# Keys times values for a pair of units and its tail in one go, in a fused attention and experts kernel

## The chip, the cores and the metric

The kernel runs on one core of one Trainium2 chip. The metric is device microseconds of one execution, the median of several. The core's engines are TensorE (PE in the profile; PEld is its weight load), VectorE (DVE), ScalarE (ACT), GpSimd (POOL) and SyncE (SP, which here issues DMAs). Each works through its own instructions in program order and waits for semaphores of the others.

## The reference

Linear attention over 4 batches, 8 heads, 576 tokens and head size 64, with 128 features, then a mixture of 8 experts (two per token), then a plain two-layer network. All is float32. The part that the change touches is `kv` and `z`:

```python
def phi(x):
    proj = np.einsum('bhsd,df->bhsf', x, w_phi)
    proj = proj - np.max(np.abs(proj), axis=-1, keepdims=True)
    return np.concatenate([np.exp(proj), np.exp(-proj)], axis=-1)
q_p, k_p = (phi(q), phi(k))
kv = np.einsum('bhsf,bhsd->bhfd', k_p, v)
z = np.sum(k_p, axis=2)
num = np.einsum('bhsf,bhfd->bhsd', q_p, kv)
den = np.einsum('bhsf,bhf->bhs', q_p, z)[..., None] + 1e-06
# x = num / den -> experts: top-2 of 8, w1, relu, w2 -> relu(x @ w_in)**2 @ w_out
```

## The kernel before

The first 290 us or so are the attention with the router's work strewn in, the rest are the experts and the last network.

A batch has 576 tokens: 512 in four rows of 128 and a tail of 64. Its keys are worked in 9 units. Unit 0 of a batch is the tail of all 8 heads; units 1 to 8 are half of a pair of heads each (pair `p`, half `f`, so units 2p + 1 and 2p + 2). One slot of the loop over `n` (line 786 on) works one unit at each stage of a pipeline written out by hand: `k_a(n + 1)` transposes keys, `k_b(n)` multiplies them with `w_phi` and lets VectorE take the maximum (`kmx`), the difference (`kd`) and ScalarE the two exponentials (`k_e`, into `kp`, or into `kpt` for a tail), and `k_c(n - 1)` adds keys times values and the sums over tokens into one bank of PSUM (`KV`), where they stay until the pair is complete; then VectorE copies the bank to `kvz`, and `k_d` turns it for the queries two slots later (`kvc`). The queries run beside: `q_a0` splits them into a high and a low part (`qhl`; ScalarE and VectorE), `q_a` transposes, `q_b` projects, POOL takes the maximum over features, `q_c1` and `q_c2` subtract and take exponentials, `q_d` multiplies with `kvc` and `norm` divides. On TensorE a slot's order is `k_a`, `q_a`, `k_b`, `q_b`, `k_d`, the router's few matmuls or none, `k_c`, `q_d`, `q_tail`.

`k_c` today: for the first unit of a pair (`f == 0`) it issues keys times values (tiles of 128 rows by 64 columns, two at once), sums (a stationary of ones, 128 by 32, four at once), then the pair's tail times values (64 by 64, since a tail's four heads of one kind have 64 partitions) and the tail's sums (64 by 32). For the second unit it issues the first two again and the copy. A unit of a tail issues nothing. A matmul of float32 shows as two passes, so `x8` in the trace are four matmuls.

The tail's values `vtt` are loaded with four heads in partitions 0 to 63 and four in 64 to 127, so a pair of heads has 64 rows. Values wait in three buffers `vt`: `load_v` (line 238, called at 796) of a pair waits on SP's queue until `k_c` has read the pair three earlier. SP's queue also holds, in program order, loads of keys and queries, the clears of the experts' input (`clear`, `xg_d<-zero`) and the experts' first weights (`w_load` in slots 6, 8, ... 20 and up, `w_conv` in the slot after, on ScalarE and VectorE).

Router: groups of tokens go through `r_0` to `r_6` over some eight slots, nearly all small VectorE work; `r_3b` puts ranks into one of the two banks `N0`, `N1` that `q_d` uses too, and `r_4` reads them.

Of the kernel before, what the change touches and what calls it, by code (L numbers as in the profile page):

```python
# [30 lines left out]
def kernel(  # L31
# [107 lines left out]
    def x_tile(pt, shape, dt, tag, small, bufs=1):  # L139
        if pt == 0:  # L140
            return xp[0].tile(shape, dt, name=tag + "0", tag=small[0], bufs=small[1])
        return xp[0].tile(shape, dt, name=tag, tag=tag, bufs=bufs)
# [5 lines left out]
    def x_load(pt):  # L148
        e, j0, j1 = parts[pt]
        if e == E - 1:  # L150
            j1 = NJ
        src = xg_d[e * CAP:e * CAP + CAP].rearrange("(j p) d -> p j d", p=128)
        if pt == 1:
            for j in range(j0, j1):
                t = stage.tile([128, DM], FT, name="xs", tag="wstage", bufs=WST)
                nc.sync.dma_start(t, src[:, j])
                XG[pt, j] = t
        else:
            t = x_tile(pt, [128, JA if pt == 0 else NJ, DM], FT, "xg", ("qhlt", 1))
            nc.sync.dma_start(t[:, :j1], src[:, :j1])  # L160
            for j in range(j1):
                XG[pt, j] = t[:, j]

    def x_t(pt, j):
        e = parts[pt][0]
        if pt not in XT:
            n = RA if pt == 0 else CAP
            XT[pt] = (x_tile(pt, [128, DC, n], FR, "xth", ("kp", 2)), x_tile(pt, [128, DC, n], FR, "xtl", ("kp", 2)))
            if pt == NP - 2:
                XT[pt + 1] = XT[pt]  # L170
        t = bank(["Tk", "M0", "M1"][j % 3], [128, DC, 128])
        for d in range(DC):
            nc.tensor.transpose(t[:, d], XG[pt, j][:, d * 128:d * 128 + 128], ident)  # L173
        c = x_cols(pt, j)
        hi_lo(XT[pt][0][:, :, c], XT[pt][1][:, :, c], t)
# [51 lines left out]
    with ExitStack() as actx:  # L227
# [26 lines left out]
            QT[b, h] = t  # L254

        def load_tails(b):
            t = ap_.tile([TL, H, D], FT, name="ktt", tag="ktt", bufs=2)
            nc.sync.dma_start(t, _ap(k, b * H * S * D + SM * D, [[D, TL], [S * D, H], [1, D]]))
            KTT[b] = t
            if b == 0:  # L260
                load_k(0, 0)
            t = ap_.tile([TL, H, D], FT, name="qtt", tag="qtt", bufs=1)
            nc.sync.dma_start(t, _ap(q, b * H * S * D + SM * D, [[D, TL], [S * D, H], [1, D]]))
            QTT[b] = t
            t = ap_.tile([128, 4, D], FT, name="vtt", tag="vtt", bufs=2)
            for s in range(2):
                nc.sync.dma_start(t[s * 64:(s + 1) * 64],
                                  _ap(v, (b * H + 4 * s) * S * D + SM * D, [[D, TL], [S * D, 4], [1, D]]))
            VTT[b] = t

# [22 lines left out]
        spare = ap_.tile([128, NTILE, 2], FT, name="spare", tag="spare")  # L293


        wf = ap_.tile([128, 128], FT, name="wf", tag="wf")
        nc.sync.dma_start(wf, _ap(w_phi, 0, [[0, 2], [128, 64], [1, 128]]))
        load_tails(0)
# [5 lines left out]
        nc.sync.dma_start(gw[:, :, 0, :], _ap(w_gate, 0, [[E, 128], [128 * E, 4], [1, E]]))  # L304
        nc.sync.dma_start(gw[:, :, 1, :], _ap(w_noise, 0, [[E, 128], [128 * E, 4], [1, E]]))

        jp = ap_.tile([128, 128], I32, name="jp", tag="jp")
        nc.gpsimd.iota(jp, pattern=[[1, 128]], base=0, channel_multiplier=-1)
        nc.vector.tensor_scalar(ident, jp, 0.0, None, op0=OP.is_equal)
        nc.scalar.activation(identr, ident, AF.Copy)  # L310
# [52 lines left out]
        def k_b(u):  # L363
            b, i = divmod(u, 9)
            hi, lo = KH.pop(u)
            t = bank(f"M{u % 2}", [128, 2, 2, 128])
            for r in range(2):
                o = t[:, r].rearrange("p h f -> p (h f)")
                s = slice(r * 128, r * 128 + 128)
                mm(o, hi[:, s], wbh, r == 0, False)  # L370
                mm(o, hi[:, s], wbl, False, False)
                mm(o, lo[:, s], wbh, False, True)
            mx = ap_.tile([128, 4], FT, name="kmx", tag="kmx", bufs=2)
            nc.vector.tensor_reduce(mx, t.rearrange("p r h f -> p (r h) f"), axis=AX.X, op=OP.max,  # L374
                                    apply_absolute_value=True)
            kd = ap_.tile([128, 4, 128], FT, name="kd", tag="kd", bufs=2)
            nc.vector.tensor_sub(kd, t.rearrange("p r h f -> p (r h) f"),
                                 mx[:, :, None].to_broadcast([128, 4, 128]))
            if i == 0:
                kp = ap_.tile([128, 4, 2, 128], FT, name="kpt", tag="kpt", bufs=1)  # L380
                KPT[b] = kp
            else:
                kp = ap_.tile([128, 4, 2, 128], FT, name="kp", tag="kp", bufs=2)
                KP[u] = kp
            KE.append((kp, kd))

# [3 lines left out]
            nc.scalar.activation(kp[:, :, 1, :], kd, AF.Exp, scale=-1.0)  # L390

        def k_c(u):
            b, i = divmod(u, 9)
            if i == 0:
                return
            p, f = divmod(i - 1, 2)
            if f == 0:
                KVB[b, p] = bank("KV", [128, 512])
            t = KVB[b, p]
            kp = KP.pop(u).rearrange("p (h r) a f -> p r h (a f)", h=2)  # L400
            for r in range(2):
                for h in range(2):
                    mm(t[h * 64:h * 64 + 64, :256], VT[b, p][:, h, 2 * f + r, :], kp[:, r, h],
                       f == 0 and r == 0, f == 1 and r == 1)
            for h in range(2):
                for r in range(2):
                    g = 32 * (2 * h + r)
                    mm(t[g:g + 32, 256:], ones32, kp[:, r, h], False, f == 1)
            if f == 0:
                rows = slice((p // 2) * 64, (p // 2) * 64 + 64)  # L410
                kt = KPT[b].rearrange("p (r h) a f -> p r h a f", h=2)
                for h in range(2):
                    mm(t[h * 64:h * 64 + 64, :256], VTT[b][rows, (p % 2) * 2 + h, :],
                       kt[rows, p % 2, h].rearrange("p a f -> p (a f)"), False, False)
                for h in range(2):
                    for a in range(2):
                        g = 32 * (2 * h + a)
                        mm(t[g:g + 32, 256 + a * 128:384 + a * 128], ones32[rows], kt[rows, p % 2, h, a], False, False)
            else:
                kvz = ap_.tile([128, 512], FT, name="kvz", tag="kvz", bufs=1)  # L420
                nc.vector.tensor_copy(kvz, t)
                KVZ[b, p] = kvz

        def k_d(u):
            b, i = divmod(u, 9)
# [15 lines left out]
        def q_a0(u):  # L441
            b, i = divmod(u, 9)
            if i == 0:
                s = ap_.tile([TL, H, 2, D], FR, name="qhlt", tag="qhlt", bufs=1)
                hi_lo(s[:, :, 0, :], s[:, :, 1, :], QTT[b])
            else:
                s = ap_.tile([128, R, 2, D], FR, name="qhl", tag="qhl", bufs=2)
                hi_lo(s[:, :, 0, :], s[:, :, 1, :], QT[b, i - 1])
            QHL[u] = s

        def q_a(u):
            b, i = divmod(u, 9)
            t = bank("Tq", [128, 512], FR)
            s = QHL.pop(u)
            if i == 0:
                for h in range(H):
                    nc.tensor.transpose(t[:, h * 64:h * 64 + 64],
                                        s[:, h].rearrange("p a d -> p (a d)"), identr[:64, :64])
            else:
                for r in range(R):  # L460
                    nc.tensor.transpose(t[:, r * 128:r * 128 + 128],  # L461
                                        s[:, r].rearrange("p a d -> p (a d)"), identr)
            o = ap_.tile([128, 512], FR, name="qtr", tag="qtr", bufs=2)
            nc.scalar.activation(o, t.bitcast(FT), AF.Copy)
            QTR[u] = o

        def q_b(u):
            t = bank("P", [128, 512])
            o = QTR.pop(u)
            mm(t, wsh, o, True, False)  # L470
            mm(t, wsl, o, False, True)
            ps = ap_.tile([128, 512], FT, name="ps", tag="ps", bufs=3)
            nc.scalar.activation(ps, t, AF.Copy)  # L473
            mx = ap_.tile([128, 512], FT, name="qmx", tag="qmx", bufs=3)
            nc.gpsimd.partition_all_reduce(mx, ps, 128, bass.bass_isa.ReduceOp.absmax)  # L475
            PS[u] = (ps, mx)

# [784 lines left out]
```

## Time and profile before

| what | us |
|---|---|
| median of three runs | 1144.59 (1144.57 to 1145.79) |
| profiled execution | 1142.34 |
| its span, first to last instruction | 1140.6 |
| TensorE busy in the span | 1101.5 (97%) |
| VectorE busy | 642.7 (56%) |
| ScalarE busy | 493.8 (43%) |
| GpSimd busy | 396.8 (35%) |
| mean granted clock of TensorE, share of full | 0.987 |

Times are of one profiled execution unless they are called medians. A matmul's end is modelled, so groups of matmuls are read from the start of one to the start of the next. A table of windows gives, for a stretch, its length and each engine's busy time in it; an engine whose busy time equals the length never waited. "Idle before" in brackets, with an arrow, is how long an engine waited and what ended the wait.

### The profile page before, as it was taken

What the parts mean: (1) busy time and instruction counts of PE and PEld (TensorE: products, weight loads), DVE (VectorE), ACT (ScalarE), POOL (GpSimd) and SP (SyncE); (2) the same over time, 40 slices, a digit from 0 to 9 for tenths busy, and PEclk for the clock granted to TensorE, in tenths of its full rate; (3) what the DMA queues carried; (4) which work ended last, traced back from release to release, by engine and by line L of the source; (5) the groups of instructions that cost most, each with busy time, mean ns of one, the idle gap of its engine ahead of it and who ended that gap; (6) DMA issues with size and microseconds to landing.
All of it is one profiled execution on the core that took longest, in us unless ns stands there. A gap on an engine that the chain in (4) does not pass through costs nothing.

```text
span 1140.6 us, 17665 instructions
## 1 busy us (share of the span) xinstructions
PE 1101.5 (97%) x6588; PEld 935.0 (82%) x6588; DVE 642.7 (56%) x1247; ACT 493.8 (43%) x1025; POOL 396.8 (35%) x374
## 2 busy tenths in 40 slices
PE   7999889989999999999999999999999999999996
PEld 4676667678889999999999988888898888888885
DVE  6778778775148687878777774343343333333222
ACT  5767567641453535444445354443233232222221
POOL 3333342743545454545454545553010010000000
PEclk9999999998999999999999999999999999999998
DMA  5768352614646555555555555332112011001001
GB/s 133 223 178 263 89 168 65 208 75 173 224 142 199 180 193 183 193 178 189 179 194 180 196 182 164 122 109 74 37 39 55 19 38 56 19 1 37 1 1 40
DMA packets 106366, 142.51 MB, mean 125 GB/s; under 512 B 17570, under 2 KB 59682, under 8 KB 105762
## 3 DMA queue, kind: packets, MB, share of 16 engines
q1 hardware_dynamic: 100514, 122.44, 33.9%
q0 software_dynamic: 5760, 18.88, 5.1%
q8 instruction: 54, 0.88, 0.3%
q14 instruction: 38, 0.31, 0.1%
HBM read 92.97 MB, written 48.31 MB: 124 GB/s over the span
## 4 chain that ended last, share of the span: by engine, by line
PE 86%; DVE 6%; DMA 2%; issue 2%; ACT 1%; another core or an unknown queue 1%; POOL 1%; SPq 0%; POOLq 0%
PE M L81 38%; PE N L81 16%; PE KV L81 12%; PE P L81 9%; PE Tq L81 8%; DVE qhl L85 1%; PE Tk L81 1%; PE Tq L461 1%; PE M L173 1%; DMA wstage<-in_moe_w_dram 1%; DVE kmx L374 1%; PE Tk L995 1%; PE Tk L173 1%; PE Tk L356 1%
## 5 line engine op out<-in xcount | busy, mean ns | idle before, releaser
L1016 DVE TENSOR_TENSOR r<-M,r 128x512 f32<-128x512 f32 (+1 forms) x80 | 51.0, 638 | 245.1 <-ACT h2h L1015 242.3
L1012 ACT ACTIVATE r<-M 128x512 f32<-128x512 f32 (+1 forms) x80 | 44.4, 555 | 247.7 <-PE M L81 245.5
L202 ACT ACTIVATE hh<-M 128x320 fp32r<-128x320 f32 (+2 forms) x128 | 50.8, 437 | 227.7 <-PE M L81 220.6
L199 DVE SCALAR_TENSOR_TENSOR hl<-M,hh 128x320 fp32r<-128x320 f32 (+2 forms) x128 | 58.1, 486 | 114.7 <-ACT hh L202 113.4
L475 POOL PARTITION_ALL_REDUCE qmx<-ps x36 | 69.9, 1942 | 137.0 <-ACT ps L473 132.7
L977 POOL DMA_INDIRECT ya<-y_d,yrows x18 | 17.9, 997 | 187.2 <-PE Tk L995 112.5
L81 PEld LDWEIGHTS N<-kvc,qp 128*128 128x128 f32 x512 | 62.1, 197 | 17.5 <-issue 11.9
L81 PE MATMUL N<-kvc,qp 128*128 128x81 f32 x512 | 67.0, 284 | 9.5 <-issue 4.2
L1017 DVE TENSOR_TENSOR h2l<-r,h2h 128x512 fp32r<-128x512 f32 (+1 forms) x80 | 57.7, 721 | 7.3 <-DVE r L1016 0.5
L1015 ACT ACTIVATE h2h<-r 128x512 fp32r<-128x512 f32 (+1 forms) x80 | 47.1, 589 | 2.6
L81 PE MATMUL M<-x,w30h 128*128 128x512 f32 (+1 forms) x160 | 45.9, 371 | 0.0
L81 PE MATMUL M<-x,w20h 128*128 128x512 f32 (+1 forms) x160 | 45.7, 370 | 0.0
L81 PE MATMUL M<-x,w10h 128*128 128x512 f32 (+1 forms) x160 | 45.7, 370 | 0.0
L81 PE MATMUL M<-x,w00h 128*128 128x512 f32 (+1 forms) x160 | 45.4, 368 | 0.0
L128 POOL TENSOR_TENSOR w30l<-wstage,w30h 128x512 fp32r<-128x512 f32 x20 | 27.4, 1370 | 49.9 <-ACT w30h L127 47.4
L128 POOL TENSOR_TENSOR w20l<-wstage,w20h 128x512 fp32r<-128x512 f32 x20 | 28.0, 1399 | 45.0 <-ACT w20h L127 29.4
L740 POOL DMA_INDIRECT xg_d<-x,slots x32 | 31.9, 997 | 21.7 <-DVE slots L701 11.8
L85 DVE TENSOR_TENSOR qhl<-qt,qhl 128x256 fp32r<-128x256 f32 x32 | 37.0, 1156 | 0.4 <-ACT qhl L84 0.4
L128 POOL TENSOR_TENSOR w10l<-wstage,w10h 128x512 fp32r<-128x512 f32 x16 | 22.3, 1394 | 40.6 <-ACT w10h L127 36.8
L947 POOL TENSOR_TENSOR wd<-wd 128x256 f32<-128x256 f32 x32 | 23.7, 741 | 36.0 <-DVE wd L943 31.7
L947 POOL TENSOR_TENSOR wx<-wx 128x256 f32<-128x256 f32 x32 | 23.7, 740 | 35.1 <-DVE wx L943 31.6
L952 DVE SCALAR_TENSOR_TENSOR wd<-wd 128x256 f32<-128x256 f32 x32 | 35.1, 1096 | 1.1
(439 smaller groups left out, 3465.0 us busy)
## 6 DMA issues: line engine op xcount, KB each, us to landing
wstage<-in_moe_w_dram SPq DMA_DIRECT2D x128, 256.0 KB
xg_d<-zero SPq DMA_DIRECT2D x8, 1280.0 KB
y_d<-y SPq DMA_DIRECT2D x40, 256.0 KB
xg<-xg_d SPq DMA_DIRECT2D x7, 1280.0 KB
wide<-in_moe_w_in_dram SPq DMA_DIRECT2D x32, 256.0 KB
wide<-in_moe_w_out_dram SPq DMA_DIRECT2D x32, 256.0 KB
kt<-in_k_dram SPq DMA_DIRECT2D x16, 256.0 KB
vt<-in_v_dram SPq DMA_DIRECT2D x16, 256.0 KB
```

Source lines behind the costliest of these rows:

```text
L81: nc.tensor.matmul(o, l, r, start=start, stop=stop, skip_group_check=True)
L85: nc.vector.tensor_sub(lo, src, hi.bitcast(FT))
L128: (nc.gpsimd if n >= 2 else nc.vector).tensor_sub(lo[:, c], src, hi[:, c].bitcast(FT))
L199: nc.vector.scalar_tensor_tensor(hl[:, c0:c1], o, 0.0, hh[:, c0:c1].bitcast(FT), op0=OP.max, op1=OP.subtract)
L202: nc.scalar.activation(hh[:, c[1]:c[2]], c[0], AF.Relu)
L475: nc.gpsimd.partition_all_reduce(mx, ps, 128, bass.bass_isa.ReduceOp.absmax)
L947: nc.gpsimd.tensor_mul(part, part, exp)
L952: nc.vector.scalar_tensor_tensor(exp, ok, TINY * TINY, exp, op0=OP.is_ge, op1=OP.mult)
L1012: nc.scalar.activation(r[:, :n], t[:, :n], AF.Relu)
L1015: nc.scalar.activation(hh[:, :n], r[:, :n], AF.Square)
L1016: nc.vector.tensor_mul(r[:, :n], t[:, :n], r[:, :n])
L1017: nc.vector.tensor_sub(hl[:, :n], r[:, :n], hh[:, :n].bitcast(FT))
```

## The change

`k_c` does nothing in the first unit's slot. In the second unit's slot it does both units and the tail: keys times values of the first unit, of the second, of the tail, then sums of the first, of the second, of the tail, then the copy. The tail's values now lie in two tiles of 128 partitions by 8 heads that are filled with zeros once; heads 0 to 3 are loaded into partitions 0 to 63 and heads 4 to 7 into 64 to 127, so the tail's matmuls run over all 128 rows, and rows of the other heads meet zeros. The ones of the tail's sums have zeros in the other half in the same way (`onesp`).

For this, `kp` gets a third buffer and `kpt` a second. Room is found elsewhere: `ktt` one buffer in place of two, `qmx` two in place of three, `jp` shares `kvz`'s place, and the tail's split queries take the two `qhl` buffers in two halves in place of a tile of their own (`qhlt`); the first expert's rows, which used `qhlt`'s place, now use one of `kp`'s.

```diff
-            t = x_tile(pt, [128, JA if pt == 0 else NJ, DM], FT, "xg", ("qhlt", 1))
+            t = x_tile(pt, [128, JA if pt == 0 else NJ, DM], FT, "xg", ("kp", 3))
...
-            t = ap_.tile([128, 4, D], FT, name="vtt", tag="vtt", bufs=2)
+            t = vtp[b % 2]
             for s in range(2):
-                nc.sync.dma_start(t[s * 64:(s + 1) * 64],
+                nc.sync.dma_start(t[s * 64:(s + 1) * 64, 4 * s:4 * s + 4],
                                   _ap(v, (b * H + 4 * s) * S * D + SM * D, [[D, TL], [S * D, 4], [1, D]]))
             VTT[b] = t
...
+        vtp = [ap_.tile([128, H, D], FT, name="vtp", tag=f"vtp{i}") for i in range(2)]
+        onesp = ap_.tile([128, 2, 32], FT, name="onesp", tag="onesp")
+        for t in vtp:
+            nc.gpsimd.memset(t, 0.0)
+        nc.gpsimd.memset(onesp, 0.0)
+        for s in range(2):
+            nc.gpsimd.memset(onesp[s * 64:s * 64 + 64, s], 1.0)
...
         def k_c(u):
             b, i = divmod(u, 9)
-            if i == 0:
+            if i == 0 or i % 2:
                 return
-            p, f = divmod(i - 1, 2)
-            if f == 0:
-                KVB[b, p] = bank("KV", [128, 512])
-            t = KVB[b, p]
-            kp = KP.pop(u).rearrange("p (h r) a f -> p r h (a f)", h=2)
-            for r in range(2):
+            p = (i - 1) // 2
+            t = bank("KV", [128, 512])
+            kps = [KP.pop(u - 1 + f).rearrange("p (h r) a f -> p r h (a f)", h=2) for f in range(2)]
+            kt = KPT[b].rearrange("p (r h) a f -> p r h a f", h=2)[:, p % 2]
+            for f in range(2):
+                for r in range(2):
+                    for h in range(2):
+                        mm(t[h * 64:h * 64 + 64, :256], VT[b, p][:, h, 2 * f + r, :], kps[f][:, r, h],
+                           f == 0 and r == 0, False)
+            for h in range(2):
+                mm(t[h * 64:h * 64 + 64, :256], VTT[b][:, 2 * p + h], kt[:, h].rearrange("p a f -> p (a f)"), False, True)
+            for f in range(2):
                 for h in range(2):
-                    mm(t[h * 64:h * 64 + 64, :256], VT[b, p][:, h, 2 * f + r, :], kp[:, r, h],
-                       f == 0 and r == 0, f == 1 and r == 1)
+                    for r in range(2):
+                        g = 32 * (2 * h + r)
+                        mm(t[g:g + 32, 256:], ones32, kps[f][:, r, h], False, f == 1)
...
+            for h in range(2):
+                for a in range(2):
+                    g = 32 * (2 * h + a)
+                    mm(t[g:g + 32, 256 + a * 128:384 + a * 128], onesp[:, p // 2], kt[:, h, a], False, True)
+            kvz = ap_.tile([128, 512], FT, name="kvz", tag="kvz", bufs=1)
+            nc.vector.tensor_copy(kvz, t)
+            KVZ[b, p] = kvz
...
-                s = ap_.tile([TL, H, 2, D], FR, name="qhlt", tag="qhlt", bufs=1)
-                hi_lo(s[:, :, 0, :], s[:, :, 1, :], QTT[b])
+                s = [ap_.tile([TL, R, 2, D], FR, name="qhlt", tag="qhl", bufs=2) for _ in range(2)]
+                for i in range(2):
+                    hi_lo(s[i][:, :, 0, :], s[i][:, :, 1, :], QTT[b][:, i * R:i * R + R])
```

## Rows read from the trace of the kernel before

**Rows 1.** The page, part 1: busy us, share of span, instructions.

```profile
PE 1101.5 (97%) x6588; PEld 935.0 (82%) x6588; DVE 642.7 (56%) x1247; ACT 493.8 (43%) x1025; POOL 396.8 (35%) x374
```

**Rows 2.** Windows at slots' starts: length, PE, PEld, DVE, ACT, POOL busy, clock, DMA share, GB/s.

```profile
16.09:34.94 18.85, 18.05 (x154) 10.89 (x153) 14.78 (x21) 14.65 (x32) 7.78 (x4) 1.00 0.55 154
34.94:60.83 25.89, 25.89 (x233) 19.43 (x232) 19.42 (x37) 18.57 (x38) 7.76 (x4) 1.00 0.71 210
65.36:71.60 6.24, 6.24 (x61) 4.35 (x59) 5.26 (x11) 4.89 (x11) 1.94 (x1) 1.00 0.21 62
90.76:117.64 26.88, 26.88 (x232) 20.35 (x231) 22.59 (x52) 18.68 (x40) 7.76 (x4) 0.96 0.76 243
117.64:154.30 36.66, 30.98 (x282) 25.25 (x281) 23.71 (x72) 17.96 (x38) 12.65 (x12) 0.86 0.30 91
154.30:167.15 12.85, 11.22 (x97) 7.71 (x97) 10.29 (x17) 8.25 (x18) 8.04 (x10) 0.99 0.73 244
167.15:191.93 24.78, 23.95 (x215) 18.60 (x213) 21.75 (x59) 17.89 (x40) 7.76 (x4) 1.00 0.33 93
191.93:198.43 6.50, 6.26 (x60) 4.33 (x59) 6.30 (x20) 4.91 (x11) 1.94 (x1) 1.00 0.00 0
203.72:223.61 19.89, 18.31 (x164) 13.21 (x163) 14.32 (x34) 12.84 (x29) 14.63 (x20) 1.00 0.68 239
228.70:234.83 6.13, 6.13 (x61) 4.50 (x59) 5.80 (x17) 3.94 (x9) 1.94 (x1) 1.00 0.03 7
```

**Rows 3.** Timeline of PE, 99 to 109 us: start, us, line, operation, out<-in, shapes.

```profile
99.00 0.40 PE L81 MATMUL P<-qtr,wsh 128*128 128x512 f32 x1
99.23 0.40 PE L81 MATMUL P<-qtr,wsl 128*128 128x512 f32 x1
99.56 1.08 PE L81 MATMUL KV<-kp,vt 128*64 128x256 f32 x8
100.58 0.64 PE L81 MATMUL KV<-kp,ones 128*32 128x256 f32 x8
101.15 2.01 PE L81 MATMUL N<-kvc,qp 128*128 128x81 f32 x16
...
107.67 0.65 PE L81 MATMUL KV<-kpt,vtt 64*64 64x256 f32 x4
108.25 0.42 PE L81 MATMUL KV<-kpt,ones 64*32 64x128 f32 x8
108.60 0.67 PE L81 MATMUL N<-kvc,qp 128*128 128x81 f32 x4
```

**Rows 4.** The chain that ended last, 30 to 35 us: start, length, what.

```profile
30.20 0.79 PE M L81 x6
...
34.31 0.79 PE M L81 x6
```

**Rows 5.** SP's timeline and, second, the chain that ended last, at 73 us.

```profile
73.29 0.38 SPq L240 DMA_DIRECT2D vt<-in_v_dram  x1
...
74.84 9.40 DMA wstage<-in_moe_w_dram
```

**Rows 6.** Timeline of PE, 119 to 160 us: waits before `q_d`.

```profile
127.49 1.98 PE L81 MATMUL N<-kvc,qp 128*128 128x81 f32 x16 [0.74 <-DVE runs L671]
...
136.83 3.09 PE L81 MATMUL N<-kvc,qp 128*128 128x81 f32 x16 [2.59 <-ACT qp L493]
...
149.76 2.44 PE L81 MATMUL N<-kvc,qp 128*128 128x81 f32 x16 [1.29 <-DVE ll L511]
```

**Rows 7.** Timeline of all engines, 0 to 17 us.

```profile
2.22 0.64 POOL L333 MEMSET gmat<- 128x648 f32 x1
...
6.05 0.66 PE L351 MATMUL Tk<-ident,ktt 64*128 64x64 f32 x4 [6.05 <-DMA ktt<-in_k_dram]
...
9.29 0.68 DVE L85 TENSOR_TENSOR qhlt<-qtt,qhlt 64x512 fp32r<-64x512 f32 x1
...
13.59 0.43 DVE L85 TENSOR_TENSOR qhl<-qt,qhl 128x256 fp32r<-128x256 f32 x1 [0.37 <-ACT qhl L84]
```

More of the change, by code (lines that the diff above doesn't have):

```diff
@@ L167, in x_t @@
             n = RA if pt == 0 else CAP
-            XT[pt] = (x_tile(pt, [128, DC, n], FR, "xth", ("kp", 2)), x_tile(pt, [128, DC, n], FR, "xtl", ("kp", 2)))
+            XT[pt] = (x_tile(pt, [128, DC, n], FR, "xth", ("kp", 3)), x_tile(pt, [128, DC, n], FR, "xtl", ("kp", 3)))
             if pt == NP - 2:
@@ L256, in load_tails @@
         def load_tails(b):
-            t = ap_.tile([TL, H, D], FT, name="ktt", tag="ktt", bufs=2)
+            t = ap_.tile([TL, H, D], FT, name="ktt", tag="ktt", bufs=1)
             nc.sync.dma_start(t, _ap(k, b * H * S * D + SM * D, [[D, TL], [S * D, H], [1, D]]))
@@ L305 @@
         nc.sync.dma_start(gw[:, :, 1, :], _ap(w_noise, 0, [[E, 128], [128 * E, 4], [1, E]]))
-        jp = ap_.tile([128, 128], I32, name="jp", tag="jp")
+        jp = ap_.tile([128, 128], I32, name="jp", tag="kvz", bufs=1)
         nc.gpsimd.iota(jp, pattern=[[1, 128]], base=0, channel_multiplier=-1)
@@ L379, in k_b @@
             if i == 0:
-                kp = ap_.tile([128, 4, 2, 128], FT, name="kpt", tag="kpt", bufs=1)
+                kp = ap_.tile([128, 4, 2, 128], FT, name="kpt", tag="kpt", bufs=2)
                 KPT[b] = kp
             else:
-                kp = ap_.tile([128, 4, 2, 128], FT, name="kp", tag="kp", bufs=2)
+                kp = ap_.tile([128, 4, 2, 128], FT, name="kp", tag="kp", bufs=3)
                 KP[u] = kp
@@ L402, in k_c @@
+            for f in range(2):
                 for h in range(2):
-                    mm(t[h * 64:h * 64 + 64, :256], VT[b, p][:, h, 2 * f + r, :], kp[:, r, h],
-                       f == 0 and r == 0, f == 1 and r == 1)
+                    for r in range(2):
+                        g = 32 * (2 * h + r)
+                        mm(t[g:g + 32, 256:], ones32, kps[f][:, r, h], False, f == 1)
             for h in range(2):
-                for r in range(2):
-                    g = 32 * (2 * h + r)
-                    mm(t[g:g + 32, 256:], ones32, kp[:, r, h], False, f == 1)
@@ L409, in k_c @@
[L409 to L422, printed above, removed]
+                for a in range(2):
+                    g = 32 * (2 * h + a)
+                    mm(t[g:g + 32, 256 + a * 128:384 + a * 128], onesp[:, p // 2], kt[:, h, a], False, True)
@@ L457, in q_a @@
                     nc.tensor.transpose(t[:, h * 64:h * 64 + 64],
-                                        s[:, h].rearrange("p a d -> p (a d)"), identr[:64, :64])
+                                        s[h // R][:, h % R].rearrange("p a d -> p (a d)"), identr[:64, :64])
             else:
@@ L473, in q_b @@
             nc.scalar.activation(ps, t, AF.Copy)
-            mx = ap_.tile([128, 512], FT, name="qmx", tag="qmx", bufs=3)
+            mx = ap_.tile([128, 512], FT, name="qmx", tag="qmx", bufs=2)
             nc.gpsimd.partition_all_reduce(mx, ps, 128, bass.bass_isa.ReduceOp.absmax)
```

## Prediction

> **What bounds the kernel now.** I read the page first: TensorE is busy 97% of the span [rows 1], so a change of its work is the first suspect. But a busy TensorE need not set the end of every stretch, so the second view is the table of busy time cut at the slots of the attention stage. I cut it where the first matmul of `q_b` starts; the slot numbers below count these cuts, slot 2 from 16.09 us, slot 36 from 234.83. Where TensorE's busy time equals the length, TensorE sets the pace (90.76 to 117.64: 26.88 of 26.88); where it is shorter, something else does (117.64 to 154.30: 30.98 of 36.66) [rows 2]. The third view is TensorE's order of time inside a slot, which gives the price of each group of matmuls [rows 3]. After about 290 us the expert stages run at TensorE's pace; the change touches nothing there, so what the attention stage wins or loses should reach the end.
>
> **What the change does to TensorE.** Read [rows 3] from start to start. Before, a pair of units issues six groups in two slots: keys times values 1.02 us (99.56 to 100.58) and sums 0.57 in each slot, and in the first also tail times values 0.58 (107.67 to 108.25) and tail sums 0.35. Together 2 x 1.59 + 0.93 = 4.11. The sizes tell what a step costs. Keys times values is 8 passes on two column tiles, four steps; tail times values is two steps of the same width: (1.02 - 0.58) / 2 = 0.22 a step of 256 columns. Both sums are two steps on four column tiles, of 256 and of 128 columns: (0.57 - 0.35) / 2 = 0.11 less, so 0.11 for 128 columns. What is left over is the same for each group: 1.02 - 0.88 = 0.14, 0.57 - 0.44 = 0.13, 0.58 - 0.44 = 0.14, 0.35 - 0.22 = 0.13. I take it for the price of changing the tile's shape.
>
> After, all sit in the second slot of the pair, in two groups of one shape each: values 8 + 2 steps, 2.20 + 0.14 = 2.34; sums 4 steps of 256 and 2 of 128 columns, 0.88 + 0.22 + 0.13 = 1.23; together 3.57. The padded tail is 128 rows deep in place of 64; no row has it with zeros, and its bounds are the tail's own 0.22 a step and that of keys times values, 128 rows deep, which is 0.22 too, so padding costs nothing. The first slot also loses the entry into the small tiles: from the last P matmul it is 0.33 (99.23 to 99.56) against 0.23 between two P matmuls, 0.10. So **a first slot is emptied of 2.52 + 0.10 = 2.62, a second slot grows by 3.57 - 1.59 = 1.98, and a pair saves 0.64**; 16 pairs: 10.2 us. That is the ceiling while TensorE is the bound.
>
> The Trainium skill, TensorEngine Tiling (Array Packing), Tiling Modes, says that changing the tiling mode drains the engine, and TensorE: Matmul & The Clock Gate, Step-by-step, puts the drain at about 128 cycles, an estimate of 53 ns at 2.4 GHz. By that, five changes fewer would save 0.27 a pair and 4.3 us in all in place of 10.2. The trace has 0.13 to 0.14 for a group, and I go by the trace.
>
> **Where it stays and where it doesn't.** An emptied slot can't be shorter than the loop that feeds it: `k_b`'s matmuls, VectorE's maximum, difference and low half of the queries, transposes, next `k_b`: 30.20 to 34.31, 4.11 us [rows 4]. Slot by slot:
>
> - 16.09 to 34.94, before the first `q_d`: 18.85, of which TensorE waits 0.80, in the two second slots of 4.11 each. Emptied slots fall to the floor, 4.11; second slots are 3.71 of work + 1.98 = 5.69. Two of each: 19.60, **+0.75**. Here the change costs.
> - 34.94 to 60.83 is all TensorE: two pairs, **-1.28**. So is 90.76 to 117.64, **-1.28**.
> - 65.36 to 71.60, an emptied slot: 6.24 - 2.62 is under the floor, so 4.11, **-2.13**.
> - 71.60 to 90.76: SP waits in `load_v` (73.29) for the buffer of values that `k_c` of this slot frees. Behind it on SP wait a load of queries, a clear of the experts' input, and the weights' load, which lands 9.40 after its issue [rows 5] and holds ScalarE in `w_conv`, and through it everything. `k_c` now frees the values after eight steps in place of four: 0.88 later, and the chain with it, **+0.88**. The three slots' saving doesn't count.
> - 117.64 to 154.30: `q_d` waits for VectorE at 127.49, 136.83 and 149.76 (0.74, 2.59 and 1.29 us) [rows 6]. The first slot's and third slot's lost matmuls only lengthen the wait (0.74 + 2.62 and 1.29 + 2.62); the second's 1.98 fits into 2.59. **0**.
> - 154.30 to 167.15: second, then first slot, with 1.63 of waiting that the longer second slot covers: 11.22 + 1.98 - 2.62 = 10.58, **-2.27**.
> - 167.15 to 191.93: second, first, second, and a slot without `k_c` (from 185.88): **+1.34**; the one wait of 0.83, in the last slot, comes from VectorE being late, which the longer slot before lets it make up: **-0.7**.
> - 191.93 to 198.43: emptied, but `q_d` shares its bank with the router's ranks as at 127.49, and VectorE has 6.30 of work in 6.50: **0**; the second slot after it **+1.98**.
> - 203.72 to 223.61: first, second, first, with 1.58 of waiting: 18.31 - 3.26 = 15.05, **-4.84**; the second slot after it **+1.98**.
> - 228.70 to 234.83: to the floor, 4.11, **-2.02**, and the last second slot **+1.98**.
>
> Sum: -5.6. To this come the small edits. The low half of the tail's queries is made in two pieces: 0.43 for a 128x256 piece on an idle POOL, 2 x 0.43 - 0.68 = **+0.2** at the start, where it is on the path [rows 7]; later slots have room. Five more memsets stand at the head of POOL's queue: two of 512 columns, each below the 0.64 of the 648-column one, and three small ones, 1.5 us or less. The identity matrix waits for them; nothing uses it before the first keys land at 6.05 [rows 7], so nothing; without that cover 1.5. SP's loads of the tail's values wait for them too; they are issued after two other loads. In other second slots SP's wait in `load_v` is 0.88 longer, and the loads of queries behind it are that much later in a slot that is 1.98 longer: nothing. VectorE's copy of the bank comes later in the second slot, but `q_d` (2.01 from 101.15 [rows 3]) still lies between it and its reader. One buffer less for the maxima lets POOL wait for a subtraction that comes earlier in the same slot: nothing. The first expert's rows now use a buffer of features, free only after slot 34's `k_c`, some 2.7 us later, used over 10 us on: nothing.
>
> **Forecast: -5.4 us.** The profiled execution took 1142.34 (span 1140.6 and 1.7 around it), so 1136.9; it lies 2.25 below the median of 1144.59, so in medians **1139.2**. My own range for it is 1136 to 1142.
>
> **Rivals.**
> - *VectorE becomes the bound.* From 90.76 on it has (22.59 + 10.29 + 21.75 + 14.32) / 13 = 5.30 us a slot [rows 2], and an emptied slot has (15.05 - 5.69) / 2 = 4.68 for TensorE. If its lag doesn't wait for the next long slot, six emptied slots take 0.62 more: -5.4 + 3.7 = -1.7, 1142.9. For it: the table's 6.30 of 6.50; against it: the long slots alternate with short ones, and its average is below TensorE's.
> - *The clock falls in the emptied slots: slower.* From 117.64 to 154.30 the granted clock averages 0.86, which is 2 x 0.14 x 36.66 = 10.3 us at the lower of the two levels (1.2 GHz), and it came with waits of 2.59 and 1.29 us [rows 2, 6]. So a wait of that kind brings some 5 us at 1.2 GHz and costs 2.6. The change makes waits of 3.4 and 3.9 us there and shorter ones in slots 2, 4, 11 and 29. Two more places than now use up the 5.4; four make +10.3 - 5.4 = +4.9, 1149.5. Against it: the 2.59 that stands before the longest slow stretch gets filled. The Trainium skill, TensorE: Matmul & The Clock Gate, HAM oscillation, warns of just such gaps between bursts.
> - *More than forecast.* If VectorE finishes earlier where TensorE feeds it earlier, and the clock stays up in that stretch (half of 10.3 us), up to -10.2 - 5.1 = -15.3, 1129.3; halfway, 1133.
> - *The shape isn't what costs.* If the 0.13 belongs mostly to something that each bank or row of steps keeps, and only 0.05 of it goes with a change, the ceiling is 4.3 and the sum +0.5: 1145.1. All four leftovers are alike for four shapes, which speaks for the shape.
>
> **How the numbers follow.** Forecast 0.54, VectorE 0.17, slower 0.10, more 0.14, shape 0.05. A measurement of this kernel tells 0.2%, 2.3 us, from no change. Forecast and the larger gain are faster, 0.68; VectorE and shape are within it, 0.22; the clock is slower, 0.10. The range runs from 1131.5, halfway into the larger gain, to 1146, past the two cases of no change, and leaves the rest out.
>
> **What would show it.** In the profile after: keys times values as one group of 16 passes and 4 of the tail without a gap between them, some 2.34 us from start to start, and sums 1.23; slots that alternate between about 4.6 and 7.5 us; slots 2 to 5 a little longer than 18.85; the weights' load in slot 12 issued some 4.1 us after the slot's start in place of 3.2. Wrong would be: the wait before `q_d` in slot 21 still there, VectorE busy to the brim in emptied slots with TensorE waiting for the low half, or the granted clock lower between 120 and 200 us than now.

## The result, and the profile after

The changed kernel takes 1155.55 us (1154.55 to 1156.8), the kernel before beside it 1144.58: a ratio of 1.0104 (1.0091 to 1.0117). It is 11 us **slower**; the forecast was 5.4 us faster, and the time lies outside the range. The profiled execution has a span of 1153.4 us, 12.8 more than before. Of these, 12.1 arise before 250.97 us, which is where the last emptied and filled pair ends (slot 36; 238.85 before); behind it the two profiles differ by 0.7.

The page's part 1 of the changed kernel (busy us, share of the span, instructions):

```profile
PE 1103.3 (96%) x6588; PEld 949.2 (82%) x6588; DVE 637.0 (55%) x1251; ACT 493.1 (43%) x1029; POOL 398.4 (35%) x379
```

TensorE's busy time did not fall; it rose by 1.8 against [rows 1], with some 10 us of work taken out. A busy matmul that takes twice as long is the first thing to look for. Was the work itself priced wrongly? The timeline of PE of the changed kernel, one second slot in the steady stretch (start, us, line, operation, out<-in, shapes), answers [rows 3]:

```profile
97.17 0.40 PE L81 MATMUL P<-qtr,wsh 128*128 128x512 f32 x1
97.41 0.40 PE L81 MATMUL P<-qtr,wsl 128*128 128x512 f32 x1
97.73 1.95 PE L81 MATMUL KV<-kp,vt 128*64 128x256 f32 x16
99.51 0.60 PE L81 MATMUL KV<-kpt,vtp 128*64 128x256 f32 x4
100.05 1.07 PE L81 MATMUL KV<-kp,ones 128*32 128x256 f32 x16
100.93 0.40 PE L81 MATMUL KV<-kpt,onesp 128*32 128x128 f32 x8
101.26 0.56 PE L81 MATMUL N<-kvc,qp 128*128 128x81 f32 x3
```

From 97.73 to 101.26 the whole of `k_c` takes 3.53; the prediction had 3.57. Values with tail 2.32 (2.34), sums 1.21 (1.23): the price is right, padding with zeros costs nothing. So the loss is in where the work went. The table of windows of the changed kernel, cut at the slots as in [rows 2] (length, PE, PEld, DVE, ACT, POOL busy, granted clock, DMA share, GB/s):

```profile
15.59:40.46 24.87, 21.01 (x153) 14.24 (x153) 13.14 (x21) 15.03 (x33) 7.84 (x4) 0.93 0.49 133
40.46:65.06 24.60, 24.60 (x232) 20.13 (x231) 20.02 (x39) 17.86 (x39) 7.76 (x4) 1.00 0.74 217
69.59:73.70 4.11, 3.69 (x32) 3.41 (x31) 4.01 (x9) 3.69 (x8) 1.94 (x1) 1.00 0.20 66
91.80:117.11 25.31, 24.75 (x232) 20.12 (x231) 21.43 (x54) 18.64 (x42) 7.76 (x4) 1.00 0.89 276
117.11:152.78 35.67, 26.90 (x255) 23.82 (x253) 23.66 (x71) 17.87 (x38) 12.19 (x12) 0.89 0.30 93
152.78:169.18 16.40, 14.57 (x97) 11.59 (x97) 8.76 (x17) 8.93 (x18) 8.15 (x10) 0.71 0.58 201
169.18:195.18 26.00, 24.91 (x243) 20.50 (x242) 21.93 (x60) 17.51 (x39) 7.77 (x4) 1.00 0.29 82
195.18:203.23 8.05, 5.29 (x32) 4.88 (x31) 6.39 (x20) 5.32 (x11) 1.94 (x1) 0.79 0.01 2
210.46:228.68 18.22, 15.66 (x137) 13.12 (x135) 13.98 (x35) 13.35 (x29) 14.51 (x19) 0.95 0.67 241
236.49:242.75 6.26, 4.60 (x33) 4.43 (x31) 5.89 (x17) 3.96 (x9) 1.94 (x1) 0.83 0.11 43
242.75:250.97 8.22, 8.22 (x64) 5.13 (x64) 2.79 (x13) 2.23 (x4) 1.94 (x1) 0.71 0.01 2
0.00:250.97 250.97, 219.55 (x1880) 177.17 (x1881) 176.96 (x431) 155.41 (x328) 92.74 (x98) 0.93 0.50 152
```

Read the clock column. Where it says 1.00 between 40 and 117 us, the lengths are near the forecast ones (24.60 for 25.89, 4.11 for 6.24, 25.31 for 26.88). Where most is lost against the forecast, it is 0.93, 0.71, 0.79, 0.83, 0.71. In [rows 2] it is 0.86 from 117.64 to 154.30, 0.96 and 0.99 in two others, and 1.00 in the rest. The column leaves out the start, for which the profile has no clock record: there two P matmuls start 0.43 apart (15.59 and 16.02), later 0.24 (28.91 and 29.15), so the start runs at half clock too.

I split the first 36 slots of each profile into three: TensorE's **waits** (length less busy time), what it **lost to the half clock** (its busy time inside stretches granted 0.5 and inside those at the start, before the clock's first rise, halved), and the **work** that is left, as at full clock. Before: 20.9 + 12.0 + 205.9, together 238.85. After: 31.4 + 25.1 + 194.4, together 250.97. So 11.5 us of work are gone, 10.5 of it came back as waits, and 13.1 came on top from the clock. The split is an account of one execution each: a matmul at half clock can also shorten a wait behind it.

### The profile page after: what moved, and what is told of

It is laid out like the page before. It is cut to its first block, busy times and chain, and to the rows that moved or that the text cites. A ratio compares the mean times of both kernels' runs of the same rounds, so it can differ in the third digit from the quotient of the medians.

```text
span 1153.4 us, 17670 instructions
## 1 busy us (share of the span) xinstructions
PE 1103.3 (96%) x6588; PEld 949.2 (82%) x6588; DVE 637.0 (55%) x1251; ACT 493.1 (43%) x1029; POOL 398.4 (35%) x379
## 4 chain that ended last, share of the span: by engine, by line
PE 86%; DVE 6%; issue 2%; ACT 2%; DMA 2%; another core or an unknown queue 1%; POOL 1%; SPq 0%; POOLq 0%; ACTq 0%
PE M L81 37%; PE N L81 16%; PE KV L81 12%; PE P L81 9%; PE Tq L81 8%; DVE qhl L85 1%; PE M L173 1%; DVE kmx L383 1%; PE Tq L468 1%; PE Tk L81 1%; DMA wstage<-in_moe_w_dram 1%; PE Tk L365 1%; PE Tk L1002 1%; PE Tk L173 1%
## 5 line engine op out<-in xcount | busy, mean ns | idle before, releaser
L81 PE MATMUL N<-kvc,qp 128*128 128x81 f32 x512 | 70.3, 292 | 16.7 <-DVE runs L678 6.0
L81 PEld LDWEIGHTS N<-kvc,qp 128*128 128x128 f32 x512 | 65.9, 206 | 20.3 <-issue 9.5
L747 POOL DMA_INDIRECT xg_d<-x,slots x32 | 31.9, 996 | 22.0 <-DVE slots L708 12.1
L81 PE MATMUL KV<-kp,vt 128*64 128x256 f32 x256 | 35.8, 428 | 0.0
```

Source lines behind the costliest of these rows:

```text
L747: st = nc.gpsimd.indirect_dma_start(out=xg_d, out_offset=bass.IndirectOffsetOnAxis(ap=slots[:, T0[g] + i, c:c + 1], axis=0), in_=src, in_o ...
```

## The experiments

Every run has the kernel before beside it on the same chip, and ratios are against that. In the set of four runs `fill_first`, `late_copy`, `hybrid` and `split_fill`, what follows the 36 slots takes 892.8 to 894.8 us in every profile, in all others 901.7 to 903.2, and the kernel before beside them takes 1134.11; microseconds of the whole compare only within that set. Ratios and the length of the 36 slots are used across sets; each length is that of one profiled execution.

| kernel | ratio to before | 36 slots, us | waits | lost to half clock | work |
|---|---|---|---|---|---|
| before | 1 | 238.85 | 20.9 | 12.0 | 205.9 |
| the change | 1.0104 (1.0091 to 1.0117) | 250.97 | 31.4 | 25.1 | 194.4 |
| `shape_only` | 0.9939 (0.9916 to 0.9962) | 235.66 | 21.0 | 13.5 | 201.2 |
| `split` | 0.9918 (0.9892 to 0.9945) | 233.42 | 20.1 | 14.6 | 198.8 |
| `moved_unmerged` | 1.0101 (1.0055 to 1.0148) | 253.80 | 28.7 | 21.4 | 203.8 |
| `filler` | 1.0075 (1.0055 to 1.0096) | 248.11 | 19.5 | 8.6 | 220.1 |
| `fill_first` | 0.9954 (0.9939 to 0.9969) | 232.78 | 17.3 | 5.5 | 210.0 |
| `late_copy` | 1.0407 (1.0375 to 1.044) | 289.81 | 42.2 | 54.0 | 193.6 |
| `hybrid` | 0.9909 (0.9879 to 0.9939) | 230.72 | 20.4 | 13.8 | 196.5 |
| `split_fill` | 0.9912 (0.9892 to 0.9932) | 227.19 | 17.3 | 7.7 | 202.2 |
| `after_again` | 1.0099 (1.0071 to 1.0126) | 246.58 | 32.6 | 19.1 | 195.0 |
| `hybrid_fill` | 0.9905 (0.9887 to 0.9923) | 225.34 | 17.7 | 6.0 | 201.7 |

### The two halves of the change apart

The change does two things: it joins steps of one shape, and it moves the first unit's work into the second slot. `shape_only` joins without moving, so that each unit's steps stay in its slot (the functions hold the steps of `k_c`; in the code here and below, `...` stands for what is left out):

```diff
...
+            if f == 0:
+                values(0)
+                tail_values()
+                sums(0)
+                tail_sums()
+            else:
+                values(1)
+                sums(1)
...
```

> The change with its small edits and the padded tail, but the work stays in its slots: in a pair's first slot values of the first unit, tail values, sums, tail sums; in its second slot values and sums of the second unit. So two changes of the tile's shape fewer a pair and no emptied slot (2.25 us of these groups in the first slot in place of 2.52, 1.59 in the second as before). Theory of the emptied slots (clock or waits): no loss is left, 16 x 0.27 = 4.3 us less than the kernel before, 1140, and the granted clock falls no more often than before. If the small edits (buffers, memsets, queries in two halves) were what costs: near the changed kernel's 1155.5.

Measured: 1138.53 us beside 1144.7, 0.9939. Joining alone, two changes of shape fewer a pair, takes 4.7 us of work out and shortens the slots by 3.2. The small edits are in it too, so they are not what loses.

`moved_unmerged` does the other half: all in the second slot, in the old order of shapes.

```diff
...
+            if f == 1:
+                values(0)
+                sums(0)
+                tail_values()
+                tail_sums()
+                values(1)
+                sums(1)
...
```

> All in the second slot as in the change, but in the old order, so that the shape changes as often as before (values, sums, tail values, tail sums, values, sums). If the change of shape costs 0.13 to 0.14 us: three changes more than the changed kernel in each pair, 4.0 us a group in place of 3.5, up to 16 x 0.4 = 6.5 us more, 1160 to 1162. If shape doesn't cost: as the changed kernel, 1155.5. Either way slower than before by the emptied slots.

Measured: 1158.33, 1.0101. The whole lies between the two expectations and can't be told from the change; PE's timeline of one pair can:

```profile
43.84 1.08 PE L81 MATMUL KV<-kp,vt 128*64 128x256 f32 x8
44.85 0.64 PE L81 MATMUL KV<-kp,ones 128*32 128x256 f32 x8
45.42 0.65 PE L81 MATMUL KV<-kpt,vtp 128*64 128x256 f32 x4
46.01 0.42 PE L81 MATMUL KV<-kpt,onesp 128*32 128x128 f32 x8
46.36 1.08 PE L81 MATMUL KV<-kp,vt 128*64 128x256 f32 x8
47.38 0.64 PE L81 MATMUL KV<-kp,ones 128*32 128x256 f32 x8
47.95 2.01 PE L81 MATMUL N<-kvc,qp 128*128 128x81 f32 x16
```

From 43.84 to 47.95 the six groups take 4.11, where the two of the change take 3.53: 0.58 for four changes of shape more (the expectation counts three), 0.15 each, and 9.4 us in the account of all slots. That confirms the price of a shape that the prediction took from [rows 3], and refutes the rival that the shape isn't what costs. The 36 slots are 15.0 longer than before: **moving is what loses**, and joining takes 2.8 off it in one profile of the change and 7.2 in the other (`after_again`).

`split` joins most and balances the two slots: values in their own slots, the tail's values in the first, all sums in the second.

```diff
...
+            if f == 0:
+                values(0)
+                tail_values()
+            else:
+                values(1)
+                sums(0)
+                tail_sums()
+                sums(1)
...
```

> Half of the move: values of the first unit and of the tail in the first slot (10 steps less 4: 6 x 0.22 + 0.14 = 1.46 us in place of 2.52), then values of the second unit and all sums in the second slot (1.02 + 1.23 = 2.25 in place of 1.59). Three changes of shape fewer a pair than before. Both theories: up to 16 x 0.40 = 6.4 us less than before, 1138 to 1141, since the first slots keep some work; the clock theory says the 1.2 GHz stretches stay at about the number of the kernel before, the theory of waits that the waits before q_d grow by 1.06 in slots 20, 22 and 29.

Measured: 1137.85, 0.9918. It beats both kernels, and its profile has three stretches at half clock in the 36 slots, as many as the kernel before.

### Is it the clock, or are the waits enough?

Seven stretches of the changed kernel between 32 and 248 us have the granted clock at half, 1.2 in place of 2.4 GHz, besides the start. The table of windows, cut at these stretches (columns as above):

```profile
32.50:35.90 3.40, 3.40 (x18) 2.56 (x18) 1.69 (x3) 2.14 (x6) 0.00 (x0) 0.50 1.00 273
128.00:131.40 3.40, 3.40 (x35) 3.25 (x36) 1.11 (x4) 0.00 (x0) 0.00 (x0) 0.51 0.02 5
148.50:155.30 6.80, 6.80 (x33) 5.58 (x34) 2.60 (x7) 2.66 (x6) 0.67 (x1) 0.50 0.43 135
162.20:169.00 6.80, 6.80 (x35) 6.80 (x34) 3.96 (x6) 4.35 (x9) 1.94 (x1) 0.50 0.74 234
199.70:203.10 3.40, 3.40 (x20) 3.40 (x20) 2.00 (x5) 1.29 (x3) 0.00 (x0) 0.50 0.02 5
227.00:230.40 3.40, 3.40 (x17) 2.54 (x17) 3.25 (x6) 2.76 (x8) 1.26 (x1) 0.50 0.29 116
240.70:247.50 6.80, 6.80 (x33) 4.64 (x34) 3.45 (x17) 2.70 (x5) 1.94 (x1) 0.50 0.00 0
```

TensorE is busy all through each of them, 34 us of matmuls that are 17 us of work. Now the seven longest waits in PE's timeline of the same kernel behind the start (in brackets how long, and what ended it; the eighth is 1.09):

```profile
32.20 0.48 PE L365 MATMUL Tk<-ident,kt 128*128 128x128 f32 x2 [1.61 <-ACT kvc L442]
...
126.96 2.27 PE L81 MATMUL N<-kvc,qp 128*128 128x81 f32 x14 [3.26 <-DVE runs L678]
...
147.72 2.10 PE L81 MATMUL N<-kvc,qp 128*128 128x81 f32 x12 [3.80 <-DVE ll L518]
...
161.85 0.64 PE L81 MATMUL Tk<-gmat,kvz 128*128 128x162 f32 x2 [1.83 <-issue]
...
198.57 2.21 PE L81 MATMUL N<-kvc,qp 128*128 128x81 f32 x14 [2.76 <-DVE runs L678]
...
226.62 0.44 PE L365 MATMUL Tk<-ident,kt 128*128 128x128 f32 x2 [1.72 <-issue]
...
239.67 2.81 PE L81 MATMUL N<-kvc,qp 128*128 128x81 f32 x16 [1.66 <-ACT kvc L442]
```

Seven waits, seven stretches, each beginning 0.3 to 1.1 us after the start of the matmul that ended the wait. That is a coincidence in time; the runs had to show that the one makes the other, and what it is worth. `filler` was meant to put thrown-away matmuls into the emptied slots, so that TensorE has something to do in them.

```diff
...
+            if i % 2:
+                t = bank("KV", [128, 512])
+                kp = KP[u].rearrange("p (h r) a f -> p r h (a f)", h=2)
+                for _ in range({1: 2, 3: 2, 19: 3, 21: 3, 28: 2, 34: 1}.get(u, 0)):
+                    for r in range(2):
+                        for h in range(2):
+                            mm(t[h * 64:h * 64 + 64, :256], VT[b, (i - 1) // 2][:, h, r, :], kp[:, r, h], r == 0, r == 1)
...
```

> The changed kernel with matmuls that are thrown away in six emptied slots (2, 4, 20, 22, 29 and 35: the first unit's values 2, 2, 3, 3, 2 and 1 times over, 0.88 us each at full clock), at k_c's old place. Clock theory: the waits are filled, the stretches at 1.2 GHz at 32, 128, 148, 162 and 200 us go and the first rise of the clock comes some 7 us earlier; more work and yet 6 to 11 us less, 1145 to 1150. Theory of waits (the emptied slots only show what VectorE and ScalarE need anyway): the same 1155.5 or up to 4 us more.

Measured: 1153.2, 1.0075, between the two theories, nearer to the waits. I first read it so: the clock is restored (8.6 us lost to it in place of 25.1) and it bought only 3 us. The account of its slots shows why this reading is wrong: work rose by 25.7 against the changed kernel, which is twice what was meant. The lines had also gone into `k_d`, which has the same test of the unit at its head, so the same 13 sets of eight passes stood in the second slots, where TensorE hardly ever waits. There the 13 sets are 12.7 us of work on TensorE's path. The run shows the clock restored and says nothing on what that is worth.

`fill_first` has them in the first slots alone, as in the diff above, with `{1: 2, 3: 1, 19: 3, 21: 3, 23: 1, 28: 2, 32: 2, 34: 1}`: 15 sets, 120 passes (the expectation counts one too many).

> The changed kernel, with matmuls thrown into eight emptied first slots only (2, 4, 20, 22, 24, 29, 33, 35): 16 sets of eight passes, some 15.6 us of work at full clock, in slots in which TensorE waits 19.7 us together in the changed kernel's profile; the bank they fill is not read. The run called filler put the same sets into the second slots too, where nothing waits, so that 13 sets there (12.7 us) hid what the clock gave. By my accounting of the changed kernel's first 36 slots against before (12.1 us longer: 13.1 us more at half clock, 10.5 us more waiting, 11.5 us less work) the clock is the larger half of the loss. Clock theory: half-clock stretches fall from 44 us to about 20, and with the sets lying in the waits the time falls by 9 to 13, to 1142 to 1147. Waits theory (VectorE's and POOL's chains set the slots' ends, the clock only follows): 1151 or more, the sets only taking the place of waits.

Measured: 1128.66 beside 1134.11, 0.9954. Against the ratio of the change this is 1.5%, 17 us, for matmuls that nobody reads; more than the 9 to 13 that I had expected of the clock. Its windows (stretches 2 to 5, 19 to 22, 23 to 24, 36, and all 36 slots):

```profile
15.88:36.41 20.53, 19.93 (x178) 13.36 (x178) 14.55 (x22) 15.12 (x33) 7.78 (x4) 1.00 0.54 150
114.03:146.19 32.16, 28.87 (x302) 23.62 (x301) 23.54 (x71) 17.46 (x38) 12.64 (x12) 1.00 0.31 93
146.19:158.01 11.82, 11.29 (x106) 8.46 (x105) 10.78 (x17) 8.81 (x20) 7.97 (x10) 1.00 0.77 252
226.82:232.78 5.96, 5.96 (x64) 4.09 (x64) 4.60 (x14) 2.23 (x4) 1.94 (x1) 1.00 0.01 3
0.00:232.78 232.78, 215.50 (x2000) 171.03 (x2001) 181.79 (x431) 154.96 (x328) 92.99 (x98) 1.00 0.55 163
```

The clock is 1.00 in all of them; what the account still has as lost, 5.5, is the start. Slot 36 shows it without any sum: the same 64 passes, TensorE busy from end to end in both, 8.22 in the changed kernel at 0.71, and 5.96 here. The waits themselves are not resolved: 17.3 plus 15.6 of thrown-away work is 32.9, against 31.4 in the changed kernel. Only what follows them is gone, and 18.2 us with it (13.8 against the change's second profile, `after_again`). **The clock theory holds**; that the waits alone set the time is refuted.

`late_copy` was to test another suspicion: in the changed kernel VectorE's copy of the bank waits up to 5.0 us for the long group (4.98 before 249.30), and may hold up VectorE's queue. It moves the copy one slot on, behind the maximum and difference.

```diff
-            nc.vector.tensor_copy(kvz, t)
-            KVZ[b, p] = kvz
+            KVB[b, p] = t
...
+            if 0 <= n - 2 < NU:
+                k_c2(n - 2)
             if 2 <= u < NU:
                 q_a0(u)
```

(`k_c2` holds the two lines taken out.)

> The changed kernel with VectorE's copy of the finished bank issued one slot later, behind the subtraction for the queries, the low half of the keys, the maximum and the difference, and ahead of the low half of the queries. In the changed kernel this copy stands in VectorE's queue while TensorE works on the long group (waits of up to 5.0 us), with that work behind it. Queue theory: the eight or so starved second slots get 0.7 to 1.3 shorter each, 5 to 10 us in all, 1146 to 1151. Clock theory: what stands behind the copy needs matmuls that come after the long group anyway, so within 2 us of the changed kernel, 1153.5 to 1157.5; slot 4 and its like may even get longer, since k_d waits for the copy.

Measured: 1.0407, far outside both. Slots 3 and 5 are no shorter by the 0.7 to 1.3 of the queue theory (6.88 and 6.91, after 7.40 and 6.10), and everywhere else something new happened. PE's timeline in slot 6, and the window of slots 6 to 9, where the changed kernel had no wait at all:

```profile
43.51 0.51 PE L81 MATMUL Tk<-gmat,kvz 128*128 128x162 f32 x2 [1.73 <-DVE kvz L434]
...
41.15:75.80 34.65, 31.19 (x232) 26.19 (x231) 17.87 (x37) 18.64 (x39) 7.96 (x4) 0.80 0.53 154
```

`k_d` now waits about 1.73 for the copy in fifteen pairs. Two such waits in these four slots are 3.46; the four slots are 10.05 longer than 24.60. The rest is the clock, 6.83 by the account, at 0.80. So this run, a miss by both theories, is the cleanest measurement of the price: **here a wait of 1.73 us cost 5.0**. It isn't the price of every such wait. Behind three of the fifteen (slots 13, 33 and 35) the profile has no half clock, and slot 13 is 1.9 longer than in the changed kernel (6.47 for 4.54), little more than the wait:

```profile
99.19 0.51 PE L81 MATMUL Tk<-gmat,kvz 128*128 128x162 f32 x2 [1.73 <-DVE kvz L434]
...
96.83:103.30 6.47, 4.74 (x41) 4.33 (x39) 4.33 (x10) 4.01 (x9) 1.94 (x1) 1.00 1.01 233
```

Whether the queue order costs something by itself was not settled by this run; nothing in the other runs needs it.

### Where moving is free, and the best version

`hybrid` moves work only in the pairs of slots 6 to 9, 11 to 18 and 26 to 27, and splits the others.

```diff
...
+            if (b, p) in ((0, 2), (0, 3), (1, 0), (1, 1), (1, 2), (1, 3), (2, 3)):
+                if f == 1:
+                    values(0)
+                    values(1)
+                    tail_values()
+                    sums(0)
+                    sums(1)
+                    tail_sums()
...
```

> Work moved into the second slot as in the change, but only for the pairs in slots 6 to 9, 11 to 18 and 26 to 27, in which TensorE has hardly any waits; all other pairs as in the run called split. If moving work is free wherever TensorE is the bound, and only the emptied slots that TensorE then waits in lose, this is split less some 0.25 a pair: 1135.5 to 1138, with no new half-clock stretch before 117 us. If moving costs in every slot (VectorE behind the long group), it loses there too: 1141 or more.

Measured: 1123.54 beside 1134.11, 0.9909, and 230.72 for the 36 slots, 2.7 below `split`. Of these, 0.85 lie in slots 6 to 18; 0.74 lie in slots 2 to 5, where the two kernels are the same, so differences of that size come by themselves. In slots 6 to 18 it has the lengths of the changed kernel (76.89 there, 76.64 in the change, 77.74 in `split`), and no new half-clock stretch before 117 us. Moving costs nothing there; against `split` the whole times can't be told apart.

`split_fill` puts thrown-away sets into slots 20 and 22 of `split`, which still wait.

```diff
...
             if f == 0:
+                for _ in range({19: 2, 21: 2}.get(u, 0)):
+                    for r in range(2):
+                        for h in range(2):
+                            mm(t[h * 64:h * 64 + 64, :256], VT[b, p][:, h, r, :], kps[0][:, r, h], r == 0, r == 1)
                 values(0)
...
```

> The run called split with two sets of eight thrown-away passes (1.95 us) in each of slots 20 and 22, where TensorE waits 1.8 and 2.4 us ahead of q_d and the records show the half clock. Clock theory: the half-clock stretches between 120 and 155 us (17 us) shrink to about half, the time falls by 2 to 4, to 1134 to 1136. Waits theory: no gain, 1137.5 to 1140.

Measured: 1123.46 beside 1134.11, and 36 slots in 227.19, 6.2 below `split`, 6.9 less lost to the clock: more than expected. The whole doesn't show it, 0.9912. Part of it comes back behind the 36 slots: what follows them takes 894.5 us, and 892.8 in `hybrid` of the same set. Here a stretch at half clock begins at 268.6 us, 0.9 behind the end of a wait of 1.46; `hybrid` has the same wait and no such stretch. Where the rest went stays open. Two last runs:

> The changed kernel once more, beside the kernel before on the same chip, since the last four runs had a chip whose kernel before is some 10 us quicker behind the attention stage. If the loss belongs to the attention stage, the ratio is that of the first comparison, 1.009 to 1.012, and the first 36 slots take 250 to 252 us.

Measured: 1153.57 beside 1143.36, 1.0099, as expected. The 36 slots took 246.58, not the 250 to 252 expected and 4.4 less than in the first profile, with waits and work all but unchanged (32.6 and 195.0) and 6.1 less lost to the clock. So of one and the same kernel the clock takes a different toll in different executions, 7 to 13 us more than before in the two that I have. The wait of 1.61 in slot 4, for one, has 3.4 us at half clock behind it in the first profile and none in this one:

```profile
30.82 0.44 PE L365 MATMUL Tk<-ident,kt 128*128 128x128 f32 x2 [1.61 <-ACT kvc L442]
...
30.80:40.00 9.20, 9.18 (x88) 7.05 (x89) 6.57 (x11) 7.29 (x16) 2.95 (x3) 1.00 0.98 290
```

What else decides whether the clock falls behind a wait stays open.

> hybrid and split_fill together: work moved into the second slot only where TensorE hardly waits, the other pairs split, and two thrown-away sets in each of slots 20 and 22. split_fill's 36 slots took 227.2 us, hybrid's other stretches 1.2 to 2.5 less than split's: 225 to 226.5 here, and a ratio of 0.988 to 0.991. If moving work and keeping TensorE busy work on the same microseconds, it is no better than split_fill: 0.991 or more.

Measured: 1131.81 beside 1143.36, 0.9905, and 225.34 for the 36 slots, each as expected; the whole can't be told from `split_fill`. It has the shortest attention stage of all, 25.6 us below the first profile of the change. I would keep `split` or `hybrid`, which need no thrown-away work.

## Why the prediction was wrong

| slots | forecast | the change | of it clock | of it waits | `fill_first` |
|---|---|---|---|---|---|
| 2 to 5 | +0.75 | +6.0 | +4.7 | +3.1 | +1.7 |
| 6 to 9 | -1.28 | -1.3 | 0 | 0 | -1.3 |
| 10 to 14 | -1.25 | -3.2 | -0.5 | -1.4 | -2.2 |
| 15 to 18 | -1.28 | -1.6 | -1.2 | +0.6 | -1.6 |
| 19 to 22 | 0 | -1.0 | -1.2 | +3.1 | -4.5 |
| 23 to 24 | -2.27 | +3.6 | +4.6 | +0.2 | -1.0 |
| 25 to 28 | +0.64 | +1.2 | 0 | +0.3 | +1.2 |
| 29 to 30 | +1.98 | +3.5 | +1.7 | +2.5 | +1.9 |
| 31 to 34 | -2.86 | +1.1 | +1.7 | +1.0 | -1.2 |
| 35 to 36 | -0.04 | +4.3 | +3.4 | +1.7 | +1.2 |
| all, with the start | -5.4 | +12.1 | +13.1 | +10.5 | -6.1 |

(All columns are us against the kernel before, `fill_first` as a length. What clock and waits leave of the change's column is work.)

**The price of the work was right**: 3.53 for 3.57, 0.64 a pair, slots that alternate between 4.53 and 7.6 to 7.8, -1.29 for -1.28 in slots 6 to 9. The Trainium skill, TensorEngine Tiling (Array Packing), Tiling Modes, has the engine drain at each change of mode. `moved_unmerged` agrees that a change costs time, at 0.15 us each in place of the prediction's estimate of 53 ns; that it is the drain, no run shows.

**The step that failed is the one that counted a wait at its own length.** "An emptied slot can't be shorter than the loop that feeds it" gave 4.11 [rows 4], and "the lost matmuls only lengthen the wait" gave nothing. The waits came as forecast where I had worked them out: 3.26 in slot 20 (0.74 + 2.62), 0.64 left in slot 21, 3.80 in slot 22 (1.29 + 2.62), 2.76 in slot 29. What I did not put into the sum is that the matmuls behind each of the long ones ran at half clock: the clock took 13.1 us more than before, to which the sum gave nothing. It stood among the rivals, with its mechanism and nearly its time: four more places, 1149.5; the first profile has four more stretches than before and a later rise at the start. That 1149.5 falls short by 6 has two causes: the clock took 13.1 in place of the rival's 10.4, and the sum missed waits, as told below. I gave it 0.10, and named a lower clock between 120 and 200 us as the sign of being wrong; there it is, 0.89 and 0.71. The argument against it, that the longest of the old waits gets filled, was true (slot 21) and weighed one place gained against six that I had listed myself. [rows 6] already had the price: waits of 2.59 and 1.29, and a stretch at 0.86 around them [rows 2]. With `fill_first`, where the clock stays up, the 36 slots come out 6.1 us shorter than before. That this is near the forecast of -5.4 is luck: stretch by stretch the two differ by up to 4.5 (slots 19 to 22), `fill_first` also wins back 6.5 of the 12.0 us that the kernel before loses to the clock, and it holds 15.6 us of work that the forecast knew nothing of.

**Waits that the sum missed.** At before's clock loss the change would by the account have won 1.0 (12.1 - 13.1), not 5.4. Three places carry most of the rest, and the waits in them (slots 24, 33 and 35) stood neither in the sum nor among the rival's six. In slots 23 to 24 I let the longer second slot cover 1.63 of waiting; 1.83 is left, in slot 24. In slots 31 to 34 I let 1.58 of waiting vanish; after the change it was 2.56, all in slot 33. Most of it, 1.72 before 226.62, comes after the slot's own matmuls, and the profile names no releaser ("issue"); ScalarE's copy to `kvc`, which frees that bank, starts only at 226.12, about when GpSimd's scatters of the experts' rows end (226.32). Whether the scatters hold it up is a guess, not tested. What is shown is that the waits of the emptied slot grew, from 1.14 to 2.56: I had counted it as slack without asking what ends it. In slot 35 `q_d` waits 1.66 for `kvc`: `k_d`, the copy by ScalarE and `q_d` are a chain, and `k_c` used to stand between the first and the last on TensorE. I had looked for who waits behind the filled slots and not for what the emptied work had covered.

**The small edits.** The start became 0.5 shorter, not 0.2 longer. The weights' load went out at 77.78, 4.1 after its slot's start, as forecast:

```profile
77.78 3.36 SPq L116 DMA_DIRECT2D wstage<-in_moe_w_dram  x1
```

But it held up less: TensorE waits 0.69 in slot 14 against 2.50, and slots 12 to 14 are 1.1 shorter in place of 0.9 longer. That VectorE becomes the bound is not what made the loss: it is busy to the brim in slot 11 (4.01 of 4.11), which has just the forecast length, and `fill_first`, with the same work on VectorE, has nothing left of the loss. One slip in the prediction's arithmetic changes nothing: halfway between 1139.2 and 1129.3 is 1134.2, not 1133.

## What to carry to other kernels

Work taken out of a stage that TensorE doesn't fill is not saved but turned into a wait, and a wait in front of dense matmuls can cost more than its length: here 1.73 us cost 5.0, in most places but not in all. Ask of each step that is moved away not only where the work goes but how long TensorE stands still where it was, and what it covered; a change that saves work by joining shapes should keep the slots level, as `split` does. And when a run comes out between two theories, count its instructions before reading it: `filler` had twice the work it was meant to have, and nearly acquitted the right suspect.

## What the runs showed of the hardware

- Thrown-away matmuls can shorten a kernel. 60 of them (120 passes), 15.6 us of work, made the 36 slots 18.2 us shorter than in one profile of the change and 13.8 than in the other. The Trainium skill, TensorE: Matmul & The Clock Gate, HAM oscillation, advises for matmuls of few rows that wait for transfers either to restructure the loop so that the engine stays warm, or to pad them. Here the waits are for other engines; remedies of both kinds helped: `split` loses 14.6 us to the half clock and `fill_first` 5.5, the change 25.1.
- Within one kernel the clock's toll differs from execution to execution, 25.1 and 19.1 us, with nearly equal waits (31.4 and 32.6).
- A change of shape between groups of float32 matmuls costs 0.13 to 0.15 us, and filling 64 rows up to 128 with zeros costs nothing: the tail's values and sums, each behind a change of shape, take 0.59 and 0.35 padded (`moved_unmerged`, 45.42 to 46.36) and 0.58 and 0.35 unpadded [rows 3].
